# Splitting the products of FF2 unevenly by columns: chunked attention with a rational feed-forward layer on one core

## Chip, cores and metric

The kernel runs on 1 core of one Trainium2 chip. The metric is the device time of one execution in microseconds, lower is better. Before the change it was 930.79 us, the median of 3 runs (930.73 to 931.65).

## What is computed

Attention within chunks of 64 tokens (8 batches, 8 heads, 576 tokens, head size 64), followed by a feed-forward layer with a rational function between its two matrices (512 to 2048 to 512), for 4608 tokens:

```python
scores = scale * q_c @ k_c.transpose(0, 1, 2, 4, 3)
attn = softmax(scores)                 # over chunks of 64
x = (attn @ v_c)  as 4608 x 512
h = x @ w_in                           # FF1
P = a[0] + a[1] * h + a[2] * h**2 + a[3] * h**3
Q = 1.0 + abs(b[0]) * abs(h) + abs(b[1]) * h**2
g = P / (Q + 1e-06)
out = g @ w_out                        # FF2
```

## The kernel before, in words

The 4608 tokens are cut into 18 blocks of 256 (n = 0 to 17), the 2048 hidden columns into four steps of 512 (s = 0 to 3). Every matrix of FF1 and FF2 is held as the sum of two parts, hi and lo, of the type fp32r, and a product of matrices is made as three: hi by hi, hi by lo and lo by hi. The order of the work is written out by hand: each engine does its instructions in program order. A start program (START) does the first 12 (n, s) steps, mixed with the loading and parting of the weights; from block 3 on a loop at the end of the function does one (n, s) step a turn.

A turn makes FF1 of its step (`ff1`, L318 to L329: two halves, together 48 products of 256 token columns into the tile `ph`), starts the chain on ScalarE and VectorE that makes the rational function of it (`chain_a` to `chain_glo`, which leave `ghi` and `glo`), does a piece of the attention of the block to come, and then FF2 of the step two turns back (`ff2`, L381 to L395). The attention pieces on TensorE are the scores (`pss`, 64-column products, behind FF1 of s = 0), the transposes (`pst`, 128 columns, behind the FF2 run of the turn of s = 1) and attention by values (`psx`, 64 columns, behind FF1 of s = 2). So in a block the runs of products on TensorE follow each other as: FF1 s=0, scores, FF2 s=2 of the block before, FF1 s=1, FF2 s=3 of the block before, transposes, FF1 s=2, attention by values, FF2 s=0, FF1 s=3, FF2 s=1.

An FF2 run accumulates into the two banks of `po` (i = 0, 1: 128 tokens each, 512 columns). Its three parts issue 8 products of ghi by hi and lo weights, 8 more, and 8 of glo by hi weights; a weight load of 128x128 of g goes ahead of each matmul instruction. Each of these 24 products of 512 columns is issued as two matmul instructions of 256 columns, but for four in each block: the first one into each bank (s = 0, part 0, k = 0 and 2, which starts the accumulation) and the last one into each bank (s = 3, part 2, k = 3 and 7, which stops it) are one instruction of 512 columns:

```python
            start = s == 0 and part == 0 and k in (0, 2)
            stop = s == NST - 1 and part == 2 and k in (3, 7)
            for c in ([slice(0, DM)] if start or stop else [slice(0, 256), slice(256, DM)]):
```

Of the kernel before, what the change touches and what calls it, by code (L numbers as in the profile page):

```python
# [23 lines left out]
DM = 512  # L24
DFF = 2048
FPS = 4
NST = DFF // (128 * FPS)
# [18 lines left out]
)  # L46
FIRST = 12
PL_TAG = {0: "po", 1: "p1"}

# [4 lines left out]
def tile_chunked_attention_rational_moe(  # L54
# [32 lines left out]
    def bank_pair(tag, name):  # L87
        return ps.tile([P, 2, 512], F32, tag=tag, name=name)
# [227 lines left out]
    ch, gbuf, obuf = {}, {}, {}  # L316
# [61 lines left out]
        nc.vector.tensor_mul(gbuf[n, s][1], B, A)  # L378


    def ff2(n, s, tag, part):  # L381
        if s == 0 and part == 0:
            obuf[n] = bank_pair(tag, f"po{n}")
        ghi, glo = gbuf[n, s]
        if part < 2:
            mm = [(ghi, w, fi, i) for fi in (2 * part, 2 * part + 1) for i in range(2) for w in (wo_hi, wo_lo)]
        else:
            mm = [(glo, wo_hi, fi, i) for i in range(2) for fi in range(FPS)]
        for k, (g, w, fi, i) in enumerate(mm):
            start = s == 0 and part == 0 and k in (0, 2)  # L390
            stop = s == NST - 1 and part == 2 and k in (3, 7)
            for c in ([slice(0, DM)] if start or stop else [slice(0, 256), slice(256, DM)]):
                nc.tensor.matmul(  # L393
                    obuf[n][:, i, c], g[:, fi, i * 128:(i + 1) * 128], w[:, FPS * s + fi, c], start=start, stop=stop,
                )  # L395

    def store(n, last=False):
# [50 lines left out]
    for k, letter in enumerate("Zzy"):  # L448
        do[letter] = lambda g, k=k: ff2(*steps[g], po_tag(steps[g][0]), k)
# [13 lines left out]
    total = len(steps)  # L463
    for g in range(FIRST, total + LAG):
        n, s = steps[min(g, total - 1)]
# [59 lines left out]
```

## Time and profile before

| what | value |
|---|---|
| median of 3 runs | 930.79 us (930.73 to 931.65) |
| profiled execution, its own time | 930.22 us |
| its span in the trace | 928.4 us |
| TensorE, matmuls (PE) | 886.0 us busy, 9306 instructions |
| TensorE, weight loads (PEld) | 867.7 us busy, 9306 instructions |
| VectorE (DVE) | 746.9 us busy |
| ScalarE (ACT) | 593.9 us busy |
| mean granted clock of TensorE | 0.983 of 2.4 GHz |

Matmuls are pipelined: one of 256 columns is shown with a duration of some 280 ns, but the next starts long before that is over. The rate of a stream is therefore read from the starts, and a busy share of TensorE near 100% doesn't tell how fast products follow each other. In the rows, f32 in a shape stands for fp32r too. A few records of matmuls are missing, so counts can be one or two short.

### The profile page before, as it was taken

What the parts mean: (1) busy time and instruction counts of PE and PEld (TensorE: products, weight loads), DVE (VectorE), ACT (ScalarE), POOL (GpSimd) and SP (SyncE); (2) the same over time, 40 slices, a digit from 0 to 9 for tenths busy, and PEclk for the clock granted to TensorE, in tenths of its full rate; (3) what the DMA queues carried; (4) which work ended last, traced back from release to release, by engine and by line L of the source; (5) the groups of instructions that cost most, each with busy time, mean ns of one, the idle gap of its engine ahead of it and who ended that gap; (6) DMA issues with size and microseconds to landing.
All of it is one profiled execution on the core that took longest, in us unless ns stands there. A gap on an engine that the chain in (4) does not pass through costs nothing.

```text
span 928.4 us, 20908 instructions
## 1 busy us (share of the span) xinstructions
PE 886.0 (95%) x9306; PEld 867.7 (93%) x9306; DVE 746.9 (80%) x668; ACT 593.9 (64%) x984; POOL 0.8 (0%) x8
## 2 busy tenths in 40 slices
PE   3589899999999999999999999999999999999997
PEld 2578899999999999999999999999999999999997
DVE  5788888798787878787878787878787888878774
ACT  5999688757474747475757575656565656565452
POOL 0000000000000000000000000000000000000000
PEclk9779899999999999999999999999999999999999
DMA  8443531202020202011110202020202020101011
GB/s 295 165 152 137 181 117 44 55 16 92 1 92 1 86 7 63 30 38 55 24 70 10 83 1 92 2 92 1 92 2 92 2 92 2 47 1 24 1 24 23
DMA packets 20601, 55.87 MB, mean 60 GB/s; under 512 B 2592, under 2 KB 2592, under 8 KB 20512
## 3 DMA queue, kind: packets, MB, share of 16 engines
q1 hardware_dynamic: 20512, 54.54, 18.1%
q8 instruction: 73, 1.20, 0.5%
q14 instruction: 16, 0.13, 0.0%
HBM read 45.09 MB, written 9.44 MB: 59 GB/s over the span
## 4 chain that ended last, share of the span: by engine, by line
PE 82%; ACT 12%; DVE 3%; DMA 2%; issue 1%; SPq 0%; ACTq 0%
PE po L393 39%; PE ph L329 38%; ACT raw L162 3%; PE psx L203 2%; DMA raw<-in_w_in 2%; PE pss L203 2%; ACT raw L158 1%; PE pst L282 1%; ACT e L258 1%; ACT wo_hi L169 1%; ACT A L334 1%; ACT A L349 1%; ACT C L341 1%; ACT B L337 1%; ACT A L353 1%
## 5 line engine op out<-in xcount | busy, mean ns | idle before, releaser
L329 PE MATMUL ph<-xhi,wi_hi 128*128 128x256 f32 x1152 | 326.2, 283 | 8.6 <-DVE C L361 5.2
L329 PE MATMUL ph<-xlo,wi_hi 128*128 128x256 f32 x1152 | 324.2, 281 | 1.6 <-DVE xlo L313 1.6
L329 PE MATMUL ph<-xhi,wi_lo 128*128 128x256 f32 x1152 | 323.6, 281 | 0.0
L334 ACT ACTIVATE A<-ph,ab 128x1024 f32<-128x1024 f32 x72 | 81.3, 1129 | 273.7 <-PE ph L329 272.0
L393 PE MATMUL po<-wo_hi,ghi 128*128 128x256 f32 (+1 forms) x1116 | 230.6, 285 | 3.2 <-DVE ghi L366 3.2
L329 PEld LDWEIGHTS ph<-xhi,wi_hi 128*128 128x128 f32 x1152 | 221.5, 192 | 10.1 <-issue 4.1
L393 PE MATMUL po<-wo_lo,ghi 128*128 128x256 f32 x1152 | 227.5, 279 | 0.0
L329 PEld LDWEIGHTS ph<-xlo,wi_hi 128*128 128x128 f32 x1152 | 219.3, 190 | 2.3 <-DVE xlo L313 2.2
L329 PEld LDWEIGHTS ph<-xhi,wi_lo 128*128 128x128 f32 x1152 | 219.5, 191 | 0.0
L345 DVE SCALAR_TENSOR_TENSOR B<-B,ab,A 128x1024 f32<-128x1024 f32 x72 | 92.4, 1284 | 112.9 <-ACT B L337 112.9
L393 PEld LDWEIGHTS po<-wo_lo,ghi 128*128 128x128 f32 x1152 | 177.9, 188 | 1.6
L393 PEld LDWEIGHTS po<-wo_hi,ghi 128*128 128x128 f32 x1116 | 171.1, 188 | 5.7 <-DVE ghi L366 3.4
L393 PE MATMUL po<-wo_hi,glo 128*128 128x256 f32 (+1 forms) x1116 | 146.9, 284 | 1.9 <-DVE glo L378 1.9
L393 PEld LDWEIGHTS po<-wo_hi,glo 128*128 128x128 f32 x1116 | 137.2, 189 | 3.2 <-DVE glo L378 2.4
L366 DVE SCALAR_TENSOR_TENSOR ghi<-C,ab,A 128x1024 fp32r<-128x1024 f32 x72 | 92.4, 1284 | 11.0 <-ACT A L353 2.4
L349 ACT ACTIVATE A<-B,cst 128x1024 f32<-128x1024 f32 x72 | 83.9, 1166 | 26.4 <-DVE B L345 26.3
L361 DVE SCALAR_TENSOR_TENSOR C<-C,ab,ph 128x1024 f32<-128x1024 f32 x72 | 92.2, 1280 | 3.2 <-ACT B L337 1.0
L374 DVE SCALAR_TENSOR_TENSOR B<-C,ab,B 128x1024 f32<-128x1024 f32 x72 | 92.5, 1285 | 2.4
L378 DVE TENSOR_TENSOR glo<-B,A 128x1024 fp32r<-128x1024 f32 x72 | 88.2, 1225 | 6.8
L357 DVE TENSOR_TENSOR C<-C,ph 128x1024 f32<-128x1024 f32 x72 | 87.5, 1215 | 4.5 <-ACT B L337 3.6
L370 DVE SCALAR_TENSOR_TENSOR B<-B,ghi 128x1024 f32<-128x1024 f32 x72 | 88.2, 1225 | 2.3
L341 ACT ACTIVATE C<-ph,ab 128x1024 f32<-128x1024 f32 x72 | 88.0, 1222 | 2.5 <-DVE B L374 2.3
(53 smaller groups left out, 712.4 us busy)
## 6 DMA issues: line engine op xcount, KB each, us to landing
v<-in_vP SPq DMA_DIRECT2D x18, 512.0 KB, 4.0
out<-o SPq DMA_DIRECT2D x72, 128.0 KB, 2.4
raw<-in_w_in SPq DMA_DIRECT2D x8, 1024.0 KB, 6.6
raw<-in_w_out SPq DMA_DIRECT2D x8, 1024.0 KB, 5.9
qk<-in_qT SPq DMA_DIRECT2D x16, 512.0 KB, 4.7
qk<-in_kT SPq DMA_DIRECT2D x16, 512.0 KB, 5.7
Aqk<-in_qT SPq DMA_DIRECT2D x2, 256.0 KB, 3.4
Bqk<-in_kT SPq DMA_DIRECT2D x2, 256.0 KB, 4.0
```

The source lines that it names most:

```text
L329: nc.tensor.matmul(ph[:, fi, :], w[:, cc, f], x[:, cc, :], start=(k == 0), stop=(k == len(mm) - 1))
L334: nc.scalar.activation(ch[n, s][1], ch[n, s][0], AF.Abs, scale=b0)
L341: nc.scalar.activation(ch[n, s][3], ch[n, s][0], AF.Identity, bias=a2, scale=a3)
L345: nc.vector.scalar_tensor_tensor(B, B, b1a, A, ALU.mult, ALU.add)
L349: nc.scalar.activation(A, B, AF.Ln, bias=cst[:, 0:1], scale=2.0 ** -KLN)
L357: nc.vector.tensor_mul(C, C, h)
L361: nc.vector.scalar_tensor_tensor(C, C, a1, h, ALU.add, ALU.mult)
L366: nc.vector.scalar_tensor_tensor(gbuf[n, s][0], C, a0, A, ALU.add, ALU.mult)
L370: nc.vector.scalar_tensor_tensor(B, B, CQ, gbuf[n, s][0].bitcast(F32), ALU.add, ALU.mult)
L374: nc.vector.scalar_tensor_tensor(B, C, a0, B, ALU.add, ALU.subtract)
L378: nc.vector.tensor_mul(gbuf[n, s][1], B, A)
L393: nc.tensor.matmul(obuf[n][:, i, c], g[:, fi, i * 128:(i + 1) * 128], w[:, FPS * s + fi, c], start=start, stop=stop,)
```

## The change

The first product of each FF2 run (part 0, k = 0) and the last one (part 2, k = 7) are cut at column 256 + first and 256 + last in place of 256; first and last come from a table by block and step, with values of 0 to 48 in steps of 4. The table is zero for blocks 0 to 2; of its other 120 entries 13 are zero. The products that were one instruction of 512 columns are cut in two as all others are, at 256 or at the cut of the table; the start mark stands on the first of the two alone, the stop mark on the second.

```diff
+CUTS = [
+    [(0, 0), (0, 0), (0, 0), (0, 0)],
+    [(0, 0), (0, 0), (0, 0), (0, 0)],
+    [(0, 0), (0, 0), (0, 0), (0, 0)],
+    [(20, 32), (40, 28), (12, 0), (4, 24)],
+    [(28, 0), (16, 8), (40, 4), (24, 48)],
+    [(12, 8), (20, 24), (0, 24), (48, 32)],
+    [(16, 48), (16, 8), (16, 20), (20, 4)],
+    [(16, 16), (0, 0), (24, 24), (16, 16)],
+    [(32, 40), (24, 12), (28, 28), (24, 16)],
+    [(24, 48), (32, 0), (40, 48), (16, 16)],
+    [(32, 8), (40, 32), (20, 20), (0, 20)],
+    [(28, 40), (8, 32), (40, 32), (4, 40)],
+    [(16, 4), (4, 16), (0, 32), (0, 40)],
+    [(48, 0), (12, 48), (40, 48), (20, 0)],
+    [(4, 0), (16, 20), (24, 8), (24, 4)],
+    [(40, 12), (40, 12), (32, 4), (8, 20)],
+    [(40, 32), (0, 48), (8, 24), (40, 12)],
+    [(20, 40), (16, 40), (32, 12), (8, 32)],
+]
...
+        first, last = CUTS[n][s]
         for k, (g, w, fi, i) in enumerate(mm):
-            start = s == 0 and part == 0 and k in (0, 2)
-            stop = s == NST - 1 and part == 2 and k in (3, 7)
-            for c in ([slice(0, DM)] if start or stop else [slice(0, 256), slice(256, DM)]):
+            cut = 256 + (first if part == 0 and k == 0 else last if part == 2 and k == len(mm) - 1 else 0)
+            for c in (0, 1):
+                start = s == 0 and part == 0 and k in (0, 2) and c == 0
+                stop = s == NST - 1 and part == 2 and k in (3, 7) and c == 1
+                cols = slice(cut, DM) if c else slice(0, cut)
                 nc.tensor.matmul(
-                    obuf[n][:, i, c], g[:, fi, i * 128:(i + 1) * 128], w[:, FPS * s + fi, c], start=start, stop=stop,
+                    obuf[n][:, i, cols], g[:, fi, i * 128:(i + 1) * 128], w[:, FPS * s + fi, cols], start=start, stop=stop,
                 )
```

## Rows read from the trace of the kernel before

**Rows 1.** The page, part 1: busy us, share of the span, instructions.

```profile
PE 886.0 (95%) x9306; PEld 867.7 (93%) x9306; DVE 746.9 (80%) x668; ACT 593.9 (64%) x984; POOL 0.8 (0%) x8
```

**Rows 2.** The page, part 2: granted TensorE clock in 40 slices, tenths.

```profile
PEclk9779899999999999999999999999999999999999
```

**Rows 3.** The page, part 4: the chain of waits that ended last, by line.

```profile
PE po L393 39%; PE ph L329 38%; ACT raw L162 3%; PE psx L203 2%; DMA raw<-in_w_in 2%; PE pss L203 2%; ACT raw L158 1%; PE pst L282 1%; ACT e L258 1%; ACT wo_hi L169 1%; ACT A L334 1%; ACT A L349 1%; ACT C L341 1%; ACT B L337 1%; ACT A L353 1%
```

**Rows 4.** Waits, whole span: us in total, times, longest us.

```profile
PE ph L329 <- DVE C L361: 5.2, 5, 2.2
PE po L393 <- DVE ghi L366: 3.2, 1, 3.2
```

**Rows 5.** Stretches: length, busy us by engine, clock, DMA; two blocks, the loop.

```profile
531.46:579.33 47.87, 47.87 (x519) 47.26 (x517) 38.86 (x35) 29.25 (x56) 0.00 (x0) 1.00 0.14 45
579.33:627.20 47.87, 47.87 (x518) 47.27 (x517) 38.87 (x35) 29.25 (x56) 0.00 (x0) 1.00 0.15 46
...
227.56:922.30 694.74, 694.74 (x7331) 686.55 (x7324) 558.73 (x485) 413.62 (x747) 0.00 (x0) 1.00 0.13 40
```

**Rows 6.** Stretches from second to last start of nine runs, columns as above.

```profile
586.39:591.60 5.21, 5.21 (x47) 5.21 (x47) 4.28 (x5) 4.93 (x10) 0.00 (x0) 1.00 0.01 2
591.83:597.25 5.42, 5.42 (x48) 5.42 (x47) 5.11 (x5) 3.82 (x26) 0.00 (x0) 1.00 0.01 3
597.49:602.80 5.31, 5.31 (x47) 5.26 (x45) 4.84 (x7) 4.94 (x5) 0.00 (x0) 1.00 0.00 0
604.03:609.25 5.22, 5.22 (x48) 5.22 (x47) 4.50 (x4) 1.14 (x2) 0.00 (x0) 1.00 0.66 144
610.89:616.19 5.30, 5.30 (x46) 5.25 (x44) 4.39 (x4) 5.01 (x5) 0.00 (x0) 1.00 0.32 128
616.43:621.65 5.22, 5.22 (x49) 5.22 (x47) 5.04 (x5) 0.00 (x0) 0.00 (x0) 1.00 0.02 3
621.88:627.09 5.21, 5.21 (x49) 5.21 (x47) 3.03 (x3) 4.84 (x5) 0.00 (x0) 1.00 0.00 0
627.32:632.74 5.42, 5.42 (x49) 5.42 (x47) 5.11 (x5) 0.36 (x1) 0.00 (x0) 1.00 0.00 0
203.20:208.62 5.42, 5.42 (x48) 5.42 (x47) 5.24 (x7) 3.22 (x4) 0.00 (x0) 1.00 0.02 3
```

**Rows 7.** Timeline, TensorE, start and us: lead-in of two FF2 runs.

```profile
489.33 1.16 PE L203 MATMUL pss<-qk 64*64 64x64 f32 x64
490.42 0.50 PE L393 MATMUL po<-wo_hi,ghi 128*128 128x256 f32 x2
490.75 0.39 PE L393 MATMUL po<-wo_lo,ghi 128*128 128x256 f32 x2
...
610.55 0.50 PE L393 MATMUL po<-wo_hi,ghi 128*128 128x512 f32 x1
610.89 0.40 PE L393 MATMUL po<-wo_lo,ghi 128*128 128x256 f32 x2
```

**Rows 8.** Timeline, TensorE: a fast FF1 run, then a 512-column product.

```profile
894.15 0.28 PE L329 MATMUL ph<-xhi,wi_lo 128*128 128x256 f32 x1
894.27 0.39 PE L393 MATMUL po<-wo_hi,ghi 128*128 128x512 f32 x1
894.49 0.40 PE L393 MATMUL po<-wo_lo,ghi 128*128 128x256 f32 x2
...
895.20 0.40 PE L393 MATMUL po<-wo_hi,ghi 128*128 128x256 f32 x2
895.43 0.40 PE L393 MATMUL po<-wo_lo,ghi 128*128 128x256 f32 x2
```

**Rows 9.** Groups by shape for the transposes, then the timeline behind eight of them.

```profile
L282 PE MATMUL pst<-ident,e 128*128 128x128 f32 x144 | 18.7, 273 | 1.7 <-DVE e L245 0.9 <-DVE e L273 0.7
...
603.03 1.04 PE L282 MATMUL pst<-ident,e 128*128 128x128 f32 x8
603.82 0.37 PE L329 MATMUL ph<-xhi,wi_hi 128*128 128x256 f32 x1
```

**Rows 10.** Timeline, TensorE: plain f32 products (L182) beside fp32r ones (L183).

```profile
68.46 1.06 PE L182 MATMUL pl<-raw,ident 128*128 128x512 f32 x2
68.93 0.82 PE L183 MATMUL pl<-wi_hi,nident 128*128 128x512 f32 x1
69.59 1.06 PE L182 MATMUL pl<-raw,ident 128*128 128x512 f32 x2
```

## The prediction

> **What bounds the kernel now.** I read the page's busy shares first: matmuls fill 95% of the span, VectorE 80%, ScalarE 64% [rows 1]. Then the granted clock: it dips in the first slices and stands at its upper level, 2.4 GHz, behind them [rows 2]. The chain of waits gives TensorE 82% of the end, split evenly between the FF2 line L393 and the FF1 line L329 [rows 3]. The longest sums of TensorE's waits in FF1 and FF2 are 5.2 and 3.2 us [rows 4], and none lies behind 227.56 us: from there to 922.30 it is busy 694.74 of 694.74 us, at a granted clock of 1.00 [rows 5]. One block of 256 tokens takes 47.87 us, block after block, with VectorE busy 38.9 us of it [rows 5]. So in the loop nothing but the rate at which TensorE takes its products counts, and VectorE has 9 us a block to spare, ten times what could be won per block below.
>
> That rate is the point. A block holds eight runs of products, four of FF1 and four of FF2, each of 48 products of 256 columns (where two of them are one product of 512, I count two). Starts of products, not their durations, tell the rate, since durations overlap. I set windows from the second to the last start of a run [rows 6]. In the runs without a 512-column product this is 46 products: 5.21 to 5.22 us in some runs (113.3 ns a product), 5.42 us in others (117.8 ns). The two FF2 runs that hold 512-column products (597.49 and 610.89) have 45 in 5.31 and 5.30 us, 117.9 ns. There is nothing between: **a run goes in one of two rhythms**, with the same instructions, the same clock and no wait. The step is 4.5 ns a product, 0.21 us a run. Of the eight runs of this block four are slow, and blocks repeat to 0.01 us [rows 5]. From 227.56 us, where the first cut of the change comes, to the end there are 115 such runs, 58 of them slow: 14 blocks with four of eight, and the tail. That is 58 x 0.21 = 12.2 us, 1.3% of the time, which no other view shows, because TensorE is busy either way.
>
> **What sets the rhythm.** Each product needs its own 128x128 weight load, and one load is on its way while the product before it streams, so a stream goes by the longer of load and product, plus what the hand-over costs. The transposes have half the columns and still start 109 ns apart (eight take 1.04 us in all, one alone 0.273, so seven spacings take 0.767) [rows 9]: that is the load alone. 256 columns at 2.4 GHz are 107 ns. Load and product are nearly equal, so small shifts can decide which waits for which, and the fast rhythm of 113.3 ns lies closer to the bare load. What the trace shows of shifts:
> - A long product ends in the slow rhythm. At 894.27 a fast FF1 run meets a 512-column product: it takes 0.22 us, and from 894.49 on the products stand 0.12 us apart, to the end of that run [rows 8].
> - Short products end in the fast one. After the 128-column transposes the FF1 run at 603.82 is fast from its fourth product [rows 6, 9], though the FF2 run before it was slow, and so in each block. After the 64-column products at 489.33 the FF2 run begins with two products of 256 columns in 0.33 us to the third and is fast; after the like products ahead of 610.55 it begins with a 512-column one, whose successor starts only 0.34 us later, and is slow [rows 6, 7].
> - Against it: in the start program the FF2 run at 202.98 follows the same 64-column products as 489.33 and is slow, 5.42 us from 203.20 to 208.62 [rows 6].
>
> **The change, part by part.** (1) *No 512-column products.* 72 products become 144. One takes 0.22 to 0.23 us in the fast rhythm [rows 8], two of 256 take 2 x 0.1133 = 0.227: nothing, within 0.005 us each (0.4 us in all, either sign). At the start of each block's first FF2 run it takes away the long product that stands ahead of a run in the slow rhythm. Alone it would not do: where the FF2 run has no 512-column product and is fast (621.76), the FF1 run after it is slow (627.32) [rows 6], so one run would get faster and the slow/fast order of those behind it turn over.
>
> (2) *Uneven pairs.* From block 3 on, 15 blocks x 4 steps x 2 ends = 120 places, 107 of them with a cut of 4 to 48 columns; the cuts add up to 2580 columns. The sum of columns stays 512, but a product of 256-f columns cannot go faster than its load of 109 ns [rows 9], while the one of 256+f pays its columns. Upper bound: all columns, 2580/2.4 GHz = 1.08 us. Lower bound: zero, if the longer product's surplus is made up. I take the surplus over the 10 columns (4.2 ns) by which the fast rhythm exceeds load or product: 1580 columns, **+0.66 us**.
>
> (3) *The rhythm.* Each uneven pair is a long product followed by a short one, and the one after the short one can start only when its weights are there, as after the transposes. The first pair does this at the head of an FF2 run, the last pair at its tail, ahead of the FF1 run (or of the attention products). By the rows on short products I expect a run behind a cut to go fast, and count the 13 places with a zero cut as left slow: 58 - 13 = 45 runs, 45 x 0.21 = **-9.3 us** (-9.5 with unrounded numbers; I keep 9.3). Bounds: all 58 gone, -12.2 us; a third of the 115 runs left slow (38), -4.2 us; and beyond A's own case below, no gain or a loss. (4) *Blocks 0 to 2* have no cuts, but lose their 512-column products: some five runs before 227 us may change rhythm, +-1 us, taken as zero.
>
> No wait, DMA or tile is added; VectorE and ScalarE get their inputs up to 0.8 us a block earlier, which VectorE's spare 9 us takes in [rows 5]. The sum against the profiled execution, 930.22 us (span 928.4 and 1.8 around it): -9.3 + 0.7 = 921.6. The median of the runs is 930.79, 0.6 above the profiled one, so in median terms **922.2 us**.
>
> A rule that speaks against part (1): the Trainium skill, "TensorE: Matmul & The Clock Gate", section "Back-to-back issue gap", gives a sustained spacing of about 131 ns for 512 columns and 81 ns for 128, so that wide products would be cheap per column; by a straight line between the two, an estimate, a split would cost 2 x 98 - 131 = 65 ns and 72 of them 4.7 us. The 0.22 us at 894.27 disagrees with it.
>
> **The rivals.**
> - *Half and half.* The rhythm after an uneven pair is as good as random, since the trace before has no such pair and the run at 202.98 shows the same lead-in ending slow. Then about as many runs stay slow as now, and the cuts cost their 0.7: 931.5 us, 929 to 934 by one or two spreads of 115 coins (5 runs, 1.1 us) and part (4). Chance 0.24.
> - *Narrow products fall to another rate.* No row shows a product of this type with under 256 columns. The nearest row on a slower rate is the plain f32 product of 512 columns: from 68.46 to 69.59 one of them (two records) and one product of FF2's type take 1.13 us, so it takes 0.91, four times the other's 0.22 [rows 10]. If products under 256 columns went so, the 107 of them, of 232 columns on average, would take 0.41 us for 0.11: +32 us, 962 us. It would decide from the first column under 256. Against it: the 64- and 128-column products here go at their load's pace. Chance 0.07.
> - *All slow.* The longer half works as the 512-column product does, and the shorter doesn't undo it: the 57 runs in the fast rhythm go slow, +12.0 + 0.7: 943.5 us. Chance 0.04.
> - *Wide products are cheap.* If only the number of loads counted, each split would add one load, 72 x 0.109 = 7.8 us, with the rhythm as now 939 us. The 0.22 us at 894.27 speaks against it. [...] Chance 0.02.
>
> **How the numbers follow.** My case, most runs behind a cut fast, has a chance of 0.63: 922.2 us, its own range 918.8 (all 58 gone, cuts free) to 928. The range 918.8 to 933 takes in the half case but for its top, and leaves out the three slow rivals (0.13). About 0.2%, or 1.9 us, can be told from no change here. Faster by more: 0.63 and 0.03 of the half case, 0.66. Within: 0.13 of it. Slower: 0.08 of it and 0.13, 0.21.
>
> **What would show it.** After the change a block should take some 47.2 us, with nearly all windows from second to last product at 5.21 us; a count from 227 us of about 13 runs in the slow rhythm shows step (3) right, 50 to 60 shows the half case. A pair with a cut of 48 should take 0.24 to 0.25 us for 0.227; 0.5 us shows the narrow rate. What would make it wrong: slow windows behind non-zero cuts, or VectorE as the releaser of new waits at L329.

## The result, and the profile after

The changed kernel takes **934.69 us** (median of 6 runs, 934.21 to 935.39) against 930.76 for the kernel before beside it: a ratio of 1.0041, 95% interval 1.0028 to 1.0054. It is slower by 3.9 us. The forecast was 922.2 us, in a range of 918.8 to 933.

The page of the changed kernel, parts 1, 2 and 4, answers to [rows 1 to 3]:

```profile
PE 890.4 (95%) x9378; PEld 875.3 (94%) x9378; DVE 747.1 (80%) x668; ACT 593.6 (64%) x984; POOL 0.8 (0%) x8
...
PEclk9679799999999999999999999999999999999999
...
PE po L418 39%; PE ph L350 38%; ACT raw L183 3%; PE psx L224 2%; PE pss L224 2%; ACT raw L179 2%; DMA raw<-in_w_in 1%; PE pst L303 1%; ACT e L279 1%; ACT A L355 1%; ACT wo_hi L190 1%; ACT A L370 1%; ACT B L358 1%; ACT C L362 1%; DVE B L366 1%
```

There are 72 more products, as many as the 512-column products that were parted, and 4.4 us more of matmul time; the other parts of the page hardly move. The stretches of one block and of the whole loop, from the first cut to the end, answer to [rows 5] (length; busy us and count of PE, PEld, DVE, ACT, POOL; granted clock; DMA share and GB/s):

```profile
534.00:582.35 48.35, 48.35 (x523) 47.95 (x521) 38.90 (x35) 29.27 (x56) 0.00 (x0) 1.00 0.15 45
228.41:926.62 698.21, 698.21 (x7391) 693.07 (x7384) 558.80 (x485) 413.40 (x747) 0.00 (x0) 1.00 0.13 39
```

TensorE is busy through the whole loop as before, at the same clock, and the loop takes 698.21 us for 694.74: 3.47 us of the loss lie here, and 0.85 us ahead of it, since the first cut comes at 228.41 for 227.56. A block is no longer like the next: they take from 47.72 to 48.54 us, by the starts of their first FF1 run, where each took 47.87 before.

The eight runs of the block from 534.00 us, from the third start to the last but one (44 spacings, so that the uneven pairs stay outside: 4.99 us at 113.3 ns, 5.18 at 117.8), answer to [rows 6]:

```profile
534.24:539.42 5.18, 5.18 (x47) 5.18 (x45) 4.87 (x5) 0.03 (x1) 0.00 (x0) 1.00 0.02 3
541.18:546.37 5.19, 5.19 (x46) 5.19 (x45) 4.38 (x5) 4.91 (x11) 0.00 (x0) 1.00 0.00 0
546.86:551.86 5.00, 5.00 (x47) 5.00 (x45) 4.69 (x5) 3.45 (x24) 0.00 (x0) 1.00 0.02 3
552.32:557.50 5.18, 5.18 (x46) 5.18 (x45) 4.68 (x6) 4.89 (x5) 0.00 (x0) 1.00 0.00 0
558.85:563.84 4.99, 4.99 (x47) 4.99 (x45) 4.38 (x4) 1.02 (x2) 0.00 (x0) 1.00 0.66 170
565.59:570.77 5.18, 5.18 (x46) 5.18 (x45) 4.27 (x4) 4.89 (x5) 0.00 (x0) 1.00 0.32 112
571.25:576.43 5.18, 5.18 (x46) 5.18 (x45) 5.00 (x5) 0.00 (x0) 0.00 (x0) 1.00 0.00 0
576.91:582.11 5.20, 5.20 (x47) 5.20 (x45) 3.14 (x3) 4.92 (x5) 0.00 (x0) 1.00 0.00 0
```

The two rhythms are the same two as before. Six of these eight runs are in the slow one, all four of FF2 (lines 2, 4, 6, 8) among them. Over the loop it is 72 of 115 runs, where it was 58: of FF2's runs 49 (30 before), of FF1's 23 (28 before). 14 runs more at 0.206 us are 2.9 of the 3.47 us, and 0.6 are left, for the uneven pairs. No record is missing where runs are counted: each run of FF1 and FF2 in the loop has its 48 starts in the trace, or 46 where it holds two 512-column products.

### The profile page after: what moved, and what is told of

Same layout as the page of the kernel before. It is cut to its first block, busy times and chain, and to the rows that moved or that the text cites. A ratio compares the mean times of both kernels' runs of the same rounds, so it can differ in the third digit from the quotient of the medians.

```text
span 932.6 us, 21052 instructions
## 1 busy us (share of the span) xinstructions
PE 890.4 (95%) x9378; PEld 875.3 (94%) x9378; DVE 747.1 (80%) x668; ACT 593.6 (64%) x984; POOL 0.8 (0%) x8
## 4 chain that ended last, share of the span: by engine, by line
PE 82%; ACT 11%; DVE 2%; DMA 1%; issue 1%; SPq 1%; ACTq 0%
PE po L418 39%; PE ph L350 38%; ACT raw L183 3%; PE psx L224 2%; PE pss L224 2%; ACT raw L179 2%; DMA raw<-in_w_in 1%; PE pst L303 1%; ACT e L279 1%; ACT A L355 1%; ACT wo_hi L190 1%; ACT A L370 1%; ACT B L358 1%; ACT C L362 1%; DVE B L366 1%
## 5 line engine op out<-in xcount | busy, mean ns | idle before, releaser
L418 PE MATMUL po<-wo_hi,ghi 128*128 128x256 f32 (+5 forms) x1152 | 231.6, 282 | 2.9 <-DVE ghi L387 2.9
L418 PEld LDWEIGHTS po<-wo_hi,ghi 128*128 128x128 f32 x1152 | 175.5, 188 | 5.4 <-DVE ghi L387 3.1
L418 PEld LDWEIGHTS po<-wo_lo,ghi 128*128 128x128 f32 x1152 | 175.4, 188 | 0.0
L418 PE MATMUL po<-wo_hi,glo 128*128 128x256 f32 (+6 forms) x1152 | 147.5, 280 | 1.9 <-DVE glo L399 1.9
L418 PEld LDWEIGHTS po<-wo_hi,glo 128*128 128x128 f32 x1152 | 140.6, 189 | 2.4 <-DVE glo L399 2.4
```

What stands on the lines that cost most here:

```text
L418: nc.tensor.matmul(obuf[n][:, i, cols], g[:, fi, i * 128:(i + 1) * 128], w[:, FPS * s + fi, cols], start=start, stop=stop,)
```

## The experiments

In all of them the count is that of runs in the slow rhythm among the 115 from 227 or 228 us on, read from the starts of the products; the three closing FF2 runs, which nothing parts, are one of them. A boundary is the place where one run gives way to the next. All times are medians; the ratio is to the kernel before, run beside them.

| kernel | edit | count of 115 | us | ratio (95%) |
|---|---|---|---|---|
| before | | 58 | 930.8 | |
| the change | | 72 | 934.69 | 1.0041 (1.0028 to 1.0054) |
| e1_zero | no 512-column products, no cuts | 85 | 936.89 | 1.0061 (1.0046 to 1.0077) |
| e2_first | first cuts only | 67 | 932.92 | 1.0024 (1.0013 to 1.0035) |
| e3_last | last cuts only | 58 | 931.74 | 1.0004 (0.9994 to 1.0013) |
| e4_last48 | last pair 304 + 208 everywhere | 76 | 936.02 | 1.0051 (1.0036 to 1.0066) |
| e5_rule | cuts by the table of rhythms | 15 | 923.06 | 0.9921 (0.9904 to 0.9937) |
| e6_again | the changed kernel, unaltered | 72 | 934.32 (1 run) | |
| e7_rule24 | 24 columns behind all attention | 3 | 920.33 | 0.9886 (0.9873 to 0.9900) |
| e8_rule24_all | blocks 0 to 2 too | 3 | 919.83 | 0.9879 (0.9864 to 0.9894) |
| e9_rule24_last48 | last pair 304 + 208 | 3 | 921.30 | 0.9899 (0.9885 to 0.9912) |
| e10_rule20 | 20 for 24 columns | 30 | 925.45 | 0.9942 (0.9929 to 0.9954) |
| e11_tail | other cuts in the last two blocks | 0 | 918.47 | 0.9867 (0.9850 to 0.9883) |

**The parts one by one.** Theory A says that the time follows the count, and that each boundary between two runs carries the rhythm on or turns it over. Its rivals are a price for each wide product that is parted (B), a price for the columns of the uneven pairs (C), and a slower rate of narrow products (D).

e1_zero:

```diff
-CUTS = [
-    [(0, 0), (0, 0), (0, 0), (0, 0)],
...
+CUTS = [[(0, 0)] * 4] * NB
```

> All cuts zero: only the 512-column products are gone, every FF2 product is 256 + 256. Theory A (the time follows the count of runs in the slow rhythm, and each boundary between runs carries or turns the rhythm over): 45 to 70 of the 115 runs from about 227 us are slow (58 before, 72 with the change), 929 to 933 us. Rival B (splitting the wide products is what costs, a load more for each): 933 us or more with the count of slow runs as before, and then the cuts cost little.

936.89 us lie above A's range and within B's. The count decides between them. It is not that of before, as B has it, but 85, above the 45 to 70 that I gave A, which missed too. One block of this kernel, and its eight runs as above:

```profile
534.75:583.03 48.28, 48.28 (x522) 47.89 (x521) 38.86 (x35) 29.23 (x56) 0.00 (x0) 1.00 0.15 45
...
535.00:539.99 4.99, 4.99 (x46) 4.99 (x45) 4.68 (x5) 0.03 (x1) 0.00 (x0) 1.00 0.02 3
541.74:546.92 5.18, 5.18 (x46) 5.18 (x45) 4.37 (x5) 4.89 (x11) 0.00 (x0) 1.00 0.00 0
547.39:552.57 5.18, 5.18 (x46) 5.18 (x45) 4.87 (x5) 3.47 (x24) 0.00 (x0) 1.00 0.01 3
553.05:558.23 5.18, 5.18 (x46) 5.18 (x45) 4.54 (x5) 4.89 (x5) 0.00 (x0) 1.00 0.00 0
559.58:564.57 4.99, 4.99 (x46) 4.99 (x45) 4.38 (x4) 1.02 (x2) 0.00 (x0) 1.00 0.65 170
566.32:571.50 5.18, 5.18 (x46) 5.18 (x45) 4.27 (x4) 4.89 (x5) 0.00 (x0) 1.00 0.43 168
571.97:577.15 5.18, 5.18 (x46) 5.18 (x45) 5.00 (x5) 0.00 (x0) 0.00 (x0) 1.00 0.00 0
577.63:582.81 5.18, 5.18 (x46) 5.18 (x45) 3.12 (x3) 4.89 (x5) 0.00 (x0) 1.00 0.00 0
```

Each of its blocks has six runs of eight in the slow rhythm, two more than before, and takes 48.28 us for 47.87 [rows 5]: 0.41 us, which is two times 0.206. Nothing is left for the four parted products of a block. So parting them costs nothing in itself, and 5 to 6 us by the rhythm of the runs around.

e2_first and e3_last:

```diff
+CUTS = [[(f, 0) for f, l in row] for row in CUTS]    # e2_first
+CUTS = [[(0, l) for f, l in row] for row in CUTS]    # e3_last
```

> Only the first pair of each FF2 run keeps its uneven cut, the last pair is 256 + 256. Theory A: in the changed kernel all 18 FF2 runs that came with a non-zero first cut straight behind a fast FF1 run went slow, so nearly all FF2 runs are slow here (50 or more of 58), and the FF1 runs behind them are about half slow: 75 to 85 slow runs, 934 to 937 us. Rival C (uneven pairs cost their columns, rhythm apart): half of the cuts, so about half of the 3.9 us, 932.7 us.

> Only the last pair keeps its uneven cut, the first pair is 256 + 256. Theory A: in the changed kernel FF1 runs behind a slow FF2 run with a last cut of 16 or more went fast in 21 of 24 cases, and an FF2 run without a first cut straight behind a fast FF1 run stayed fast (4 of 4), so the slow runs fall to 30 to 45: 924 to 928 us. Rival C: half of the cuts, 932.7 us.

e2_first kept 50 of 58 FF2 runs slow, as expected; but 40 of 57 FF1 runs went fast, more than half, so A's 75 to 85 runs and 934 to 937 us were missed: the count was 67 and the time 932.92 us, which is also what C gives (932.7). e3_last missed too: 58, not 30 to 45, and 931.74 us. All 15 FF2 runs straight behind an FF1 run in the fast rhythm stayed fast, as expected, but 24 of the 28 FF2 runs behind attention were slow. C fails in e2_first by the count alone, in e3_last by the time too: its 932.7 us lie above all ten runs (929.29 to 932.19). The parts do not add up: of e1_zero's 85 runs in the slow rhythm the first cuts take away 18, the last cuts 27, and both together 13.

e4_last48:

```diff
+CUTS = [[(0, 0 if n < 3 else 48)] * 4 for n in range(NB)]
```

> From block 3 on every last pair is 304 + 208, every first pair 256 + 256. Theory A: FF1 behind FF2 goes fast always (in the changed kernel 48 columns gave a fast run in 6 of 6 cases), FF2 straight behind it stays fast, FF2 behind the scores goes slow (3 of 3 there with a first cut of zero), FF2 behind the attention by values is open: 15 to 30 slow runs, all blocks alike, 921 to 925 us. Rival C: cuts cost their columns, 60 x 48 columns / 2.4 GHz = 1.2 us, 932 us. Rival D (narrow products drop to a slower rate): 60 x 0.3 = 18 us on top of B's 931, 949 us.

It missed as well: 76 runs, 936.02 us. The step of my expectation that failed is that 48 columns lead FF1 to the fast rhythm always: behind a fast FF2 run they do (43 of 43 cases in all kernels), but behind a slow one they did so here in only one of three places in each block. D is out: 60 narrow products of 208 columns would have added 18 us.

**The table.** From these traces a plain order showed. I noted for every boundary in the turns of blocks 3 to 16 (112 runs a kernel) the rhythm ahead of it, the kind of boundary, the cut and the rhythm behind it. What follows a run in the fast rhythm (F; S is slow), with the later kernels added:

| boundary | cut and rhythm behind it (cases) |
|---|---|
| FF1 straight to FF2, first cut | 0: F (171); 4, 8, 16, 20, 24, 32, 40, 48: S (29) |
| scores, then FF2, first cut | 24: F (41); 0 (34), 20 (14) and 16 other values from -16 to 64 (22): S |
| attention by values, then FF2, first cut | 24: F (58); 0 (36), 20 (16) and 7 other values (18): S |
| FF2 straight to FF1, last cut | 12, 16, 24, 28, 40, 48: F (170); 0, 8, 20: S (12) |
| transposes, then FF1, last cut | 16, 48: F (83); 0, 4, 20, 32, 40: S (9) |

In 713 cases from ten kernels no combination gave two outcomes. The cases are not 713 independent ones: there are 54 combinations of boundary and cut, 26 of them seen once, and the large numbers repeat from block to block. From a run in the slow rhythm the same boundary with the same cut can give either (FF2 straight to FF1 with a zero cut: 50 times slow, 42 times fast). That accounts for the miss of e4_last48, whose expectation for FF1 rested mostly on cases from the slow side. e3_last missed chiefly by the second and third rows: 18 of its 28 FF2 runs behind attention came from a fast FF1 run and went slow with a cut of 0.

The first row shows itself in two lead-ins of the changed kernel, both behind an FF1 run in the fast rhythm (timeline, TensorE, start and us); the first has a cut of 0 (block 7, s = 1), the second one of 24:

```profile
432.40 0.28 PE L350 MATMUL ph<-xhi,wi_lo 128*128 128x256 f32 x1
432.51 0.39 PE L418 MATMUL po<-wo_hi,ghi 128*128 128x256 f32 x2
432.74 0.39 PE L418 MATMUL po<-wo_lo,ghi 128*128 128x256 f32 x2
432.96 0.39 PE L418 MATMUL po<-wo_hi,ghi 128*128 128x256 f32 x2
...
480.29 0.28 PE L350 MATMUL ph<-xhi,wi_lo 128*128 128x256 f32 x1
480.40 0.40 PE L418 MATMUL po<-wo_hi,ghi 128*128 128x280 f32 x2
480.64 0.40 PE L418 MATMUL po<-wo_lo,ghi 128*128 128x256 f32 x2
480.88 0.40 PE L418 MATMUL po<-wo_hi,ghi 128*128 128x256 f32 x2
481.11 0.40 PE L418 MATMUL po<-wo_lo,ghi 128*128 128x256 f32 x2
```

In the first, pairs follow each other after 0.23 and 0.22 us; in the second after 0.24, 0.24 and 0.23, and so to its end.

**Cuts by the table.** e5_rule takes for each boundary a cut that keeps F; behind the scores, where none was known, each block has another value:

```diff
+LADDER = [24, 4, 8, 28, 36, 44, 48, 52, 56, 64, -4, -8, -16, -24, 24]
+CUTS = [[(0, 0)] * 4] * 3 + [[(24, 16), (0, 16), (x, 16), (0, 16)] for x in LADDER]
```

> Cuts chosen from the rhythm table of the runs so far: every last pair 272 + 240 (behind a fast FF2 run this gave a fast run in 5 of 5 cases), first pair 256 + 256 straight behind FF1 (fast stayed fast in all of 30 cases or so), 280 + 232 behind the attention by values (24 columns: fast in 2 of 2), and behind the scores, where no cut from a fast run is known to end fast, another cut in each block: 24, 4, 8, 28, 36, 44, 48, 52, 56, 64, -4, -8, -16, -24. Theory A (the next rhythm is a fixed outcome of the rhythm before, the kind of boundary and the cut): all runs fast but some or all of the 15 FF2 runs behind the scores and the few behind those: 15 to 35 slow runs of 115, 921 to 926 us. Rival E (the outcome is as good as random from one program to the next): 45 to 70 slow runs, 929 to 934 us.

15 runs, 923.06 us: as theory A had it. Of the 13 values that stand behind the scores, -16 to 64, only 24 gave the fast rhythm (the last two of the list fall in blocks where no scores come between).

> The changed kernel once more, for its trace. Theory A: the same runs are slow as in the first trace, run by run from about 228 us (72 of 115), span 932 to 934 us. Rival E: another set of slow runs, agreeing with the first in about half of the places.

e6_again is the changed kernel unaltered. All 112 runs of the loop that I named by block and step had the rhythm of the first trace, run by run, and it took 934.32 us. So the rhythm belongs to the program, not to the execution.

```diff
+CUTS = [[(0, 0)] * 4] * 3 + [[(24, 16), (0, 16), (24, 16), (0, 16)]] * 15    # e7_rule24
+CUTS = [[(24, 16), (0, 16), (24, 16), (0, 16)]] * NB                        # e8_rule24_all
+CUTS = [[(0, 0)] * 4] * 3 + [[(24, 48), (0, 48), (24, 48), (0, 48)]] * 15    # e9_rule24_last48
+CUTS = [[(0, 0)] * 4] * 3 + [[(20, 16), (0, 16), (20, 16), (0, 16)]] * 15    # e10_rule20
```

> As e5_rule, with the one cut that ended fast behind the scores (24 columns) in every block. Theory A: all of the some 112 runs behind the first cut are fast, 15 fewer slow ones than in e5_rule: 923.1 - 15 x 0.21 = 920.0 us (919 to 921). Rival E (as good as random): 45 or more slow runs, 929 us or more.

> The same cuts in blocks 0 to 2 too. In the start program the order of the runs is another, so the rule was not made for it: theory A expects the loop as in e7_rule24 if the first loop run starts fast, and the start program within 1.5 us of it either way: 918.5 to 921.5 us.

> As e7_rule24, but the last pair is 304 + 208 in place of 272 + 240. Behind a fast FF2 run 48 columns ended fast as well, so theory A expects the same rhythm in every run, and the difference in time is the price of 32 columns of surplus in 60 places: 60 x 32 / 2.4 GHz = 0.8 us if the longer product pays its columns, 0 if the stream makes them up, 18 us if products under some width drop to another rate.

> As e7_rule24, but with 20 in place of 24 columns behind the scores and the attention by values, in 30 places. Theory A: from a fast run 20 columns ended slow there in every case, so 28 to 30 FF2 runs more are slow and the FF1 runs behind them recover with the last pair's 16 columns: e7_rule24 + 28 x 0.21 = 926 us. Rival C (what counts is how uneven the pairs are): 4 columns less in 30 places, within 0.1 us of e7_rule24.

All four came within 0.6 us of what theory A said: 920.33, 919.83, 921.30 and 925.45 us. Stretches of one block, of e7_rule24 and then of e9_rule24_last48:

```profile
527.68:574.81 47.13, 47.13 (x522) 46.74 (x521) 38.88 (x35) 29.20 (x56) 0.00 (x0) 1.00 0.15 46
574.81:621.95 47.14, 47.14 (x523) 46.75 (x521) 38.88 (x35) 29.20 (x56) 0.00 (x0) 1.00 0.15 46
```

```profile
527.90:575.07 47.17, 47.17 (x522) 46.78 (x521) 38.87 (x35) 29.19 (x56) 0.00 (x0) 1.00 0.15 46
```

With all eight runs fast a block takes 47.13 us, 0.74 less than before [rows 5]; four times 0.206 would be 0.82, so its six uneven pairs, with the first few products behind them until the spacing settles, cost 0.08. In e9_rule24_last48 the longer product of four pairs a block has 32 columns more, at the same rhythm in every run, and the block is 0.04 us longer. By the starts of the products a pair costs 13 ns more where FF1 follows straight (mean of 38 pairs in either kernel) and nothing ahead of the transposes (13 pairs); 32 columns at 2.4 GHz are 13.3 ns, an estimate. So ahead of FF1 the surplus is paid in full, and the narrow product of 208 columns drops to no slower rate: the next one starts 95 ns after it. VectorE keeps its 38.9 us a block, and the block shrinks without a new wait.

e10_rule20 changes one product of each FF2 run behind attention by 4 columns and loses 5 us. The two lead-ins behind attention by values, of e7_rule24 and of e10_rule20 (timeline, TensorE):

```profile
558.34 0.50 PE L399 MATMUL po<-wo_hi,ghi 128*128 128x280 f32 x2
558.68 0.40 PE L399 MATMUL po<-wo_lo,ghi 128*128 128x256 f32 x2
558.91 0.39 PE L399 MATMUL po<-wo_hi,ghi 128*128 128x256 f32 x2
```

```profile
560.25 0.51 PE L399 MATMUL po<-wo_hi,ghi 128*128 128x276 f32 x2
560.59 0.40 PE L399 MATMUL po<-wo_lo,ghi 128*128 128x256 f32 x2
560.83 0.40 PE L399 MATMUL po<-wo_hi,ghi 128*128 128x256 f32 x2
```

The uneven pair itself takes 0.34 us in both. Only behind it do they part: 0.23 us to the next pair in the first, 0.24 in the second, and so to the end of the run.

e11_tail mends the three runs at the end, where no attention stands any more between FF1 and FF2:

```diff
+CUTS = [[(24, 16), (0, 16), (24, 16), (0, 16)]] * 16 + [[(24, 16), (0, 16), (0, 16), (0, 16)]]
+CUTS += [[(0, 16), (0, 0), (0, 0), (0, 0)]]
```

> As e8_rule24_all, with zero first cuts in the last two blocks where no attention stands between the runs any more, and zero last cuts in front of the closing FF2 runs. In e7_rule24 to e9_rule24_last48 three FF2 runs of this tail were the only slow ones, with 24 columns straight behind a fast FF1 run, which ended slow in 5 of 5 cases, while zero ended fast in 171 of 171. Theory A: the tail is fast but perhaps for the last two runs, which follow FF2 directly: 2 to 4 runs x 0.21 off 919.8 us, 919.0 to 919.4 us. Rival: the tail is bound by something else, 919.8 us.

918.47 us, with no run of the loop in the slow rhythm, a little below the expectation: the closing FF2 products, 144 in a row, were slow for the most part before and are fast here. It is the fastest kernel of the study, 1.3% below the kernel before.

## Why the prediction was wrong, point by point

**What bounds the kernel: right.** TensorE alone, with two rhythms 4.5 ns a product apart, sets the time. The counts carry the loop of every kernel. From the first start of the first cut run to the last start, 694.73 us and 0.206 us for each run more or less than 58 leave 0.01 us in e1_zero, which has no uneven pairs, up to 1.1 us in the other kernels, and 1.7 us in e9_rule24_last48, which has the most columns of surplus.

**Part (1), 512-column products: the price right, the consequence missing.** Parting them costs nothing in itself, as forecast. That the order of the rhythms behind would turn over was named, but entered the sum with nothing. Alone it takes the count from 58 to 85 (e1_zero), worth +5.6 us.

**Part (2), the uneven pairs: the size right, the reason not.** +0.66 us forecast, 0.6 left in the loop. That they agree is in part luck: the forecast took the 109 ns of a load as the least that a narrow product takes, but in e9_rule24_last48 the next product starts 95 ns after one of 208 columns, and it is the one behind that comes late (134 ns for 120 in e7_rule24; means of 38 places).

**Part (3), the rhythm: the step that failed**, -9.3 us forecast and +2.9 measured: a count of 13 was expected, and it was 72. (45 x 0.21 is 9.45 us; 9.3 comes from 0.206 us a run. The slip changes nothing.) I read [rows 7 to 9] as "a long product ends slow, a short one ends fast" and concluded that a run behind an uneven pair, whose second product is short, would go fast. For the first pair behind FF1 the opposite holds: in 29 of 29 cases a cut led from the fast rhythm to the slow one, and its absence kept it in 171 of 171. The last pair does help FF1, by values and not by sign (16 yes, 20 no). Behind the transposes, the row on which I leaned most, the fast rhythm had not come from their short products: with a fast FF2 run ahead of them and a last cut of 0, 4, 20, 32 or 40 the same eight transposes led to a slow FF1 run, in 9 of 9 cases. In the trace before, the FF2 run ahead of them was slow in each block, so that the row showed one half of a turn-over. The piece of evidence against, the run at 202.98, was the better guide: there FF1 ahead of the scores was fast, and the scores with a cut of 0 turn fast to slow, in all 34 cases.

**Part (4)**, blocks 0 to 2: the first cut comes 0.85 us later, inside the +-1 us.

**The rivals.** None was what happened. Nearest is half and half, whose 929 to 934 us end just below the 934.69 measured, but its reason is not what happened: the outcomes are fixed, and came out as 72 for a mean of 57.5. Its range rested on coins of 5 runs' spread, and the range that I gave was cut at 933 on top of it. Narrow products at another rate and cheap wide products are both refuted, by e4_last48 and e9_rule24_last48 and by e1_zero. The estimate of 65 ns for a parted product, worked out from the figures of the Trainium skill, "TensorE: Matmul & The Clock Gate", section "Back-to-back issue gap", finds no support: e1_zero's blocks leave nothing for the four that each of them holds (48.28 us are 47.87 and two times 0.206).

**What stays open.** Why there are two rhythms, and what makes 16 and 24 columns different from 20, no run here shows. The weight load and the product are nearly of one length, but that this is the cause was only argued. What the trace before does show is where the 4.5 ns lie: from 227 us on a product in the middle of a run starts 110.0 ns after its own weight load in the fast rhythm (2049 products) and 114.9 ns after it in the slow one (1983), and in both the next load starts some 3 ns behind the product.

## What to carry to other kernels

Where an engine is busy through and through, look at the spacing of its starts run by run before calling its rate fixed: two levels of it here were worth 1.3% and stood in no wait. An edit that seems to cost a few ns can turn the rhythm of everything behind it, so read its effect as a table (rhythm ahead, boundary, edit, rhythm behind) from one trace with many values, and choose by that. A pattern that repeats in each block of one trace is one observation, not fourteen.

## What the runs showed of the hardware that was not expected

- Products of 256 columns, each with its own weight load, go at 113.3 or 117.8 ns, with the same instructions at the same granted clock of 1.00. Once it has settled, a run of them keeps its rhythm to its end (the one run that turned inside, the FF2 run from 883.33 in the trace before, did so at a 512-column product), and the same program takes the same rhythms in another execution, 112 of 112.
- From the fast rhythm the next one was a fixed outcome of boundary and cut (713 of 713 cases, 54 combinations); from the slow one it is not by these alone.
- 24 columns of shift behind attention keep the fast rhythm (99 of 99 cases), 20 and 28 do not (32 of 32).
- A last pair of 304 and 208 columns costs 13 ns more than one of 272 and 240 where FF1 follows straight (38 pairs in either kernel) and nothing ahead of the transposes (13 pairs); the product behind the 208 columns starts 95 ns after it, sooner than in either rhythm.
